# Two attentions interleaved in one stream, with 32-wide PE tiles and side work placed by a list scheduler

## Chip, cores and metric

One core of one Trainium2 chip. The metric is the device time of one execution in microseconds (us), lower is better. Times are medians of the fast runs or of all runs, as stated; a run counts as slow when it is over 1.5% above the fastest of its kernel. On one core there is no second die to compare with.

The engines: PE (TensorE matmul; PEld is its weight load), ACT (ScalarE), DVE (VectorE), POOL (GpSimd), SP (SyncE, here the queue that issues the DMAs). Matmul results land in a memory called PSUM, which both kernels use as eight banks of 512 columns. PV is the product of the exps with V.

## The reference

Two independent blocks on their own inputs, side by side in the output. S = 2048 tokens, D = 1024, 32 heads of 32.

```python
# A: plain multi-head attention, not causal
q, k, v = split_heads(x @ wqkv)
p = softmax(q @ k.T * 32**-0.5)
a = merge(p @ v) @ wo

# B: four segments of 512 tokens; causal attention inside a segment, and a linear memory across segments
phi = lambda t: where(t > 0, t + 1, exp(t))
for s in range(4):
    a_dot = softmax(qs @ ks.T * scale + causal_mask) @ vs
    a_mem = (phi(qs) @ M) / (phi(qs) @ z + 1e-6)
    o_s   = g * a_mem + (1 - g) * a_dot           # g = sigmoid(beta), one per head
    M += phi(ks).T @ vs ;  z += sum(phi(ks))
b = merge(o) @ wo
out = concat([a, b], -1)
```

The exp is the big job: 32 heads x 2048 x 2048 scores in A and 32 x 4 x 512 x 512, half of them masked, in B. On 128 partitions that is 1.05 M columns for A and 0.16 M for B.

## The kernel before

It runs A to its end, then B. A head group is 4 heads (128 rows of K, Q and V). A unit is one key tile of 128 for two heads: two score matmuls over all 128 rows, with K masked so that only one head's 32 rows count, one exp over 1024 columns, two PV matmuls on 64-column tiles. V carries 32 columns of ones beside its 32, so that PV also gives the sum of the softmax.

```python
def mmS(e):                                        # scores of one unit
    for s_, h in enumerate(heads):                 # two heads, two PSUM banks
        e.matmul(K.psS[:, 1024*sbuf + 512*s_ : ... + nq],
                 KTm[:, h, P*t:P*t+P],             # K with the other heads' rows zeroed: 128 rows
                 QT[:, c_q0:c_q0+nq], start=True, stop=not causal)
    if causal: ...                                 # two more matmuls add the mask
...
e.activation(dst, src, ACT.Exp, bias=cb[:, t:t+1], scale=scale)
...
e.matmul(K.psOL[64*s_:64*s_+64, col:col+nq], VE[:, t, h, 0:64], K.PT[:, pb, ...],
         start=first_t, stop=last_t, tile_position=(0, 64*s_))
```

Projections and norms of the next head group are spread over the first two of a group's four query chunks by a fixed share per unit. At the end of a chunk the sums are permuted by matmuls, inverted by one wide reciprocal and multiplied in:

```python
cpl = self.pe_op(... K.perm[:, 2+p, :] ...)        # sort the sums' rows
c2 = self.dve_op(lambda e: e.reciprocal(K.rec[:, 0:nq], K.Lsb[:, 0:nq]), ...)   # 128x512
c3 = self.dve_op(lambda e: e.tensor_tensor(OT_dst, K.Osb[:, 0:nq], K.rec[:, 0:nq], ALU.mult), ...)
```

B's phase starts only after A's last output projection, and loads its input then.

## Time and profile before

| | before |
|---|---|
| time, median of 2 runs | 2339.85 us (2338.29 to 2341.41) |
| PE / DVE / ACT / POOL busy | 74 / 44 / 57 / 0% |
| granted PE clock, mean | 0.884 |
| A's exps, from first to last | about 62 to 1346 us |
| B | about 1420 to 2280 us |

The span in 40 equal slices of 58.5 us (second part of the profile page). Each digit is the busy share of a slice in tenths; PEclk is the granted clock of PE in tenths:

```profile
PE   4888888788788788888878884657657574756659
...
ACT  0678788788788696887899900343342424243330
...
PEclk9999999999999998999999997768677686867779
```

ACT is busy in A (slices 2 to 23) and mostly idle in B. The table of windows (columns: window, its length, busy us and number of instructions of PE, PEld, DVE, ACT and POOL, granted clock, DMA share, GB/s) puts numbers to a pure stretch of A and to B:

```profile
360.00:385.00 25.00, 21.13 (x102) 4.54 (x98) 1.29 (x2) 25.00 (x27) 0.00 (x0) 1.00 0.00 1
1420.00:2280.00 860.00, 530.19 (x3666) 275.43 (x3667) 604.83 (x856) 293.20 (x424) 0.00 (x0) 0.75 0.06 12
```

In A's pure stretch ACT is busy all of its 25 us. In B no engine is: DVE leads with 605 of 860 us, at a PE clock of 0.75.

The timeline of a pure stretch of A (columns: start, us, engine, line of the kernel, operation, output and input, count, then the idle time before it and what ended it):

```profile
298.85 8.19 ACT L533 ACTIVATE PT<-psS,cb_A 128x1024 bf16<-128x1024 f32 x8
...
300.06 0.60 PE L505 MATMUL psS<-QT_A,KTm_A 128*128 128x512 bf16 x2 [0.31 <-ACT PT L533]
...
300.59 0.62 PE L547 MATMUL psOL<-PT,VE_A 128*64 128x512 bf16 x4
...
302.06 0.61 PE L505 MATMUL psS<-QT_A,KTm_A 128*128 128x512 bf16 x2 [0.31 <-ACT PT L533]
```

One period of two units runs from 300.06 to 302.06, so a 1024-column exp costs 1.00 us when they stand back to back. PE needs about 1.7 us of those 2.0. The chain of work that ended last, as shares of the span by engine and by line, for the whole kernel:

```profile
DVE 20%; PE 17%; ACT 6%; issue 3%; SPq 1%; DMA 1%; ACTq 0%; DVEq 0%
PE psX L669 4%; ACT PT L533 4%; DVE rec L619 3%; PE psS L505 3%; DVE drec_B L1022 3%; PE psX L328 3%; PE psOL L547 1%; ACT OLsb L603 1%; PE psS L510 1%; PE psX L608 1%; DVE zp_B L906 1%; DVE KTm_B L858 1%; DVE VE_B L471 1%; DVE VE_B L473 1%; DVE V_B L469 1%
```

The two lines name only half of the span, because the chain has very many short pieces. The head of it is spread over DVE, PE and ACT, and the reciprocals L619 and L1022 of B stand among its largest single lines.

### The profile page before, as it was taken

To read this page: it belongs to the slowest core of one execution; us is meant where nothing else is said; L and a number is where in the kernel's file an instruction comes from. 1 tells how busy PE (TensorE), PEld (TensorE's weight loads), DVE (VectorE), ACT (ScalarE), POOL (GpSimd) and SP (SyncE) were. 2 spreads that over 40 slices of the span, in tenths; PEclk is the share of its full clock that TensorE was granted. 3 is DMA by queue.
4 is the path that set the end of the run, shared out by engine and by line. 5 is a ranking of instruction groups with operands and counts; after the bars stand their busy time and mean duration, and the time that the engine had idled before them with its cause. 6 is when DMAs were issued, how large, how long until landed. Compare 5 with 4: busy or idle time off the path is not lost. (4 is left out here: it accounts for less than half of the span.)

```text
span 2339.9 us, 25486 instructions
## 1 busy us (share of the span) xinstructions
PE 1743.0 (74%) x10128; PEld 663.7 (28%) x10128; DVE 1020.6 (44%) x1373; ACT 1345.2 (57%) x1458; POOL 10.4 (0%) x44
## 2 busy tenths in 40 slices
PE   4888888788788788888878884657657574756659
PEld 2332222222222222322211131433324242332324
DVE  3322312332222314223122142666767676776783
ACT  0678788788788696887899900343342424243330
POOL 1000000000000000000000000000000000000000
PEclk9999999999999998999999997768677686867779
DMA  7000000000000000000000015000000000000002
GB/s 171 14 14 1 1 14 1 1 14 1 1 14 1 1 14 1 1 1 1 1 0 1 1 59 113 14 1 14 14 0 14 0 14 1 14 1 1 1 1 72
DMA packets 95702, 35.20 MB, mean 15 GB/s; under 512 B 85344, under 2 KB 93536, under 8 KB 95584
## 3 DMA queue, kind: packets, MB, share of 16 engines
q1 hardware_dynamic: 95584, 33.57, 6.3%
q8 instruction: 81, 1.33, 0.2%
q14 instruction: 37, 0.30, 0.0%
HBM read 16.78 MB, written 8.39 MB: 11 GB/s over the span
## 5 line engine op out<-in xcount | busy, mean ns | idle before, releaser
L533 ACT ACTIVATE PT<-psS,cb_A 128x1024 bf16<-128x1024 f32 x1024 | 1048.7, 1156 | 230.3 <-PE psS L505 203.9
L505 PE MATMUL psS<-QT_A,KTm_A 128*128 128x512 bf16 x2048 | 598.9, 390 | 114.0 <-ACT PT L533 112.9
L533 ACT ACTIVATE PT<-psS,cb_B 128x1024 bf16<-128x1024 f32 (+3 forms) x256 | 188.2, 789 | 399.6 <-PE psS L510 399.5
L547 PE MATMUL psOL<-PT,VE_A 128*64 128x512 bf16 x2048 | 323.4, 396 | 4.8 <-ACT PT L533 4.8
L505 PEld LDWEIGHTS psS<-QT_A,KTm_A 128*128 128x128 bf16 x2048 | 138.5, 99 | 499.6 <-ACT PT L533 446.1
L634 DVE CAST OLsb<-psOL 128x1024 bf16<-128x1024 f32 x32 | 39.1, 1221 | 440.4 <-PE psOL L547 440.4
L505 PE MATMUL psS<-QT_B,KTm_B 128*128 128x512 bf16 (+3 forms) x512 | 143.4, 378 | 46.8 <-ACT PT L533 46.6
L328 PE MATMUL psX<-xT_B,Wsl 128*128 128x512 bf16 x512 | 130.4, 402 | 45.5 <-DMA Wsl<-in_B_wv_dram 26.8
L328 PE MATMUL psX<-xT_A,Wsl 128*128 128x512 bf16 x512 | 132.0, 386 | 28.2 <-DMA Wsl<-in_A_wqkv_dram 26.3
L547 PEld LDWEIGHTS psOL<-PT,VE_A 128*64 128x64 bf16 x2048 | 73.2, 109 | 227.8 <-issue 218.1
L471 DVE TENSOR_TENSOR VE_A<-psX,fcol_A 128x512 bf16<-128x512 f32 x32 | 22.1, 691 | 244.3 <-PE psX L368 244.3
L650 DVE RECIPROCAL rec<-rec 128x512 f32<-128x512 f32 x32 | 107.0, 3343 | 0.0
L619 DVE RECIPROCAL rec<-rec 128x512 f32<-128x512 f32 x32 | 107.0, 3343 | 0.0
L1016 PE MATMUL psX<-PQ_B,Zb_B 128*128 128x512 bf16 x24 | 12.6, 527 | 96.4 <-DVE Zb_B L1012 96.4
L510 PE MATMUL psS<-maskneg,ident 128*128 128x128 bf16 x512 | 82.9, 256 | 0.0
L1022 DVE RECIPROCAL drec_B<-drec_B 128x512 f32<-128x512 f32 x24 | 80.5, 3353 | 0.8
L328 PEld LDWEIGHTS psX<-xT_B,Wsl 128*128 128x128 bf16 x512 | 47.4, 102 | 117.7 <-issue 40.5
L603 ACT ACTIVATE OLsb<-psOL 128x1024 bf16<-128x1024 f32 x32 | 32.7, 1023 | 77.6 <-PE psOL L547 77.6
L368 PE MATMUL psX<-Wsl,xT_A 128*128 128x128 bf16 x1024 | 76.3, 234 | 0.6 <-DVE rec L642 0.6
L368 PE MATMUL psX<-Wsl,xT_B 128*128 128x128 bf16 x1024 | 72.7, 238 | 5.1 <-DVE drec_B L1019 2.5
L675 DVE CAST outsb<-psX 128x512 bf16<-128x512 f32 x64 | 44.1, 691 | 73.1 <-PE psX L669 64.3
L368 PEld LDWEIGHTS psX<-Wsl,xT_A 128*128 128x128 bf16 x1024 | 64.7, 105 | 29.0 <-issue 18.5
(123 smaller groups left out, 1484.0 us busy)
## 6 DMA issues: line engine op xcount, KB each, us to landing
out_dram<-outsb SPq DMA_DIRECT2D x64, 128.0 KB, 1.7
Wsl<-in_A_wqkv_dram SPq DMA_DIRECT2D x24, 256.0 KB, 4.4
Wo_A<-in_A_wo_dram SPq DMA_DIRECT2D x1, 2048.0 KB, 10.4
Wo_B<-in_B_wo_dram SPq DMA_DIRECT2D x1, 2048.0 KB, 15.3
Wsl<-in_B_wk_dram SPq DMA_DIRECT2D x8, 256.0 KB, 3.3
Wsl<-in_B_wq_dram SPq DMA_DIRECT2D x8, 256.0 KB, 4.1
Wsl<-in_B_wv_dram SPq DMA_DIRECT2D x8, 256.0 KB, 4.5
xT_A<-in_A_x_dram SPq DMA_TRANSPOSE x8, 5.0
```

Source lines behind the costliest of these rows:

```text
L328: ins = e.matmul(K.psX[:, 512 * b:512 * b + ncol], K.Wsl[Wb][:, i, blk, :], xT[:, i, ncol * c4:ncol * c4 + ncol], start=(i == 0), stop=(i ...
L368: ins = e.matmul(K.psX[:, 512 * b + 128 * tt:512 * b + 128 * tt + 128], xT[:, i, P * t:P * t + P], K.Wsl[Wb][:, i, blk, :], start=(i == 0) ...
L505: ins = e.matmul(K.psS[:, 1024 * sbuf + 512 * s_:1024 * sbuf + 512 * s_ + nq], KTm[:, h, P * t:P * t + P], QT[:, c_q0:c_q0 + nq], start=Tr ...
L510: ins = e.matmul(K.psS[:, 1024 * sbuf + 512 * s_:1024 * sbuf + 512 * s_ + P], K.ident[:, :], K.maskneg[:, :], start=False, stop=True)
L533: attE(e.activation(dst, src, ACT.Exp, bias=cb[:, t:t + 1], scale=scale))
L547: ins = e.matmul(K.psOL[64 * s_:64 * s_ + 64, col:col + nq], VE[:, t, h, 0:64], K.PT[:, pb, 512 * s_:512 * s_ + nq], start=first_t, stop=l ...
L603: c1 = self.act_op(lambda e: e.activation(K.OLsb[:, :, 0:nq], K.psOL[:, :].rearrange("p (a n) -> p a n", a=2)[:, :, 0:nq], ACT.Copy), wait ...
L619: c2 = self.dve_op(lambda e: e.reciprocal(K.rec[:, 0:nq], K.Lsb[:, 0:nq]), waits=[(sd, cl)])
L634: c1 = self.dve_op(lambda e: e.tensor_copy(K.OLsb[:, :, 0:nq], K.psOL[:, :].rearrange("p (a n) -> p a n", a=2)[:, :, 0:nq]), waits=waits)
L650: c2 = self.dve_op(lambda e: e.reciprocal(K.rec[:, 0:nq], K.Lsb[:, 0:nq]), waits=[(sd, cl)])
L675: cd = self.dve_op(lambda e, b=b, ob=ob: e.tensor_copy(K.outsb[:, ob, :], K.psX[:, 512 * b:512 * b + 512]), waits=wd)
L1022: cd2 = self.dve_op(lambda e: e.reciprocal(drec[:, 0:L], drec[:, 0:L]), waits=[(sd, cd1)])
```

## The change

The intent is to keep ACT fed from one end to the other: B's units, one after each unit of A, so that B's serial chains run under A's exps; less PE time for scores; exps of up to 1536 columns; and side work placed into the gaps by a list scheduler that plays the program with estimated costs when it is built. The order that it finds is static: every engine then works through its list and waits on semaphores.

The diff replaces nearly the whole file. Its core, shortened and partly put in words, with cuts marked by `...`:

```diff
-for pair in range(2): for t in range(NT): unit(two heads)      # A, then all of B
+for n in range(32):                                              # A and B alternate
+    units.append(("B", n) + ...)
+    units.append(("A", n) + ...)

+SLOTS = [(0, 1, 2), (3, 4)]     # score banks: groups of 3 and of 2
+PROJ = [5]                      # the one side bank
+OB, LB = 6, 7                   # PV output, softmax sums

-ins = e.matmul(psS..., KTm[:, h, ...], QT[...])                  # 128 rows, masked K
+hs = slice(32 * h, 32 * h + 32)
+lhsT = self.KA[b][hs, P*t:P*t+P]; rhs = self.QA[b][hs, ...]      # 32-row tiles, one head each
+ACT: activation(PT[:, s0:s0+n, 0:width], ps[:, banks[0]:banks[0]+n, 0:width], Exp, bias=cb, scale=SCALE)   # n = 2 or 3

-e.matmul(K.psOL[64*s_:64*s_+64, ...], VE[:, t, h, 0:64], ...)    # 64-column tiles, V and ones together
+for ones in (False, True):
+    for h in range(4):                                           # 32-column tiles, four heads
+        e.matmul(ps[32*h:32*h+32, LB if ones else OB, ...], ones32 or V[:, t, hs], PT[...])

-# causal mask by two matmuls; bias of the softmax by matmuls, a diagonal and DVE reductions
+POOL: affine_select(PT...)                                       # causal mask after the exp
+POOL: partition_all_reduce(cbB[:, 1:2], ..., ReduceOp.max)       cost=1.0
+POOL: tensor_scalar(cbB[:, 0:1], cbB[:, 1:2], -SCALE, ...)       cost=0.2
+POOL: tensor_tensor(Mb, Mf, maskbd); tensor_scalar(Zb, maskbd, z)    # state operands of B's memory

-reciprocal of 128x512
+four reciprocals of 128x128, so that other DVE work can come between

+def proj_T(...):
+    bank = yield ("bank",)                 # a free side bank
+    for i0 in range(0, NI, 2):
+        yield ("pe", 0)                    # a gap on PE
+        R.op("PE", two matmuls, ..., cost=0.45)
+    op = R.op("DVE", copy out of the bank, ..., cost=0.66)
+    self.bank_release(bank, op)
+# scheduler: scores first, then PV, then the side task of the best priority
...
```

Loads also change: B's weights are loaded once for each of its 32 units and B's input in four parts.

## The prediction

> **What bounds the kernel now.** It runs two attentions one after the other. In A's pure attention stretches (timeline, 360 to 385 us) ScalarE is saturated: busy 25.00 of 25 us. Its 1024-column exp has a mean of 1156 ns in the groups view, but two start every 2.01 us, so it costs 1.003 us: by that, about 0.83 ns a column plus 0.15 us an instruction (my fit). 1024 of them need 1027 us, and A takes 1285 us (60 to 1345): the loss is PE side work (projections stretch two units to 2.39 us, timeline) and gaps of 3 to 6.5 us at chunk ends and norm chains (waits). Then 56 us of output projection and 26.8 us of waiting for B's loads idle ScalarE. B (1420 to 2280) is bound by serial chains: in the table of windows DVE is busy 72%, ScalarE 36%, PE 64% at a granted clock of 0.75; the chain of waits runs through reciprocals (3.34 us each), the wide reductions and PE.
>
> **What the change does.**
> - B's exps fill under A's. Exp columns stay 1.05 M (A) + 0.16 M (B). With 3+2 banks there are about 26 instructions per A unit and 5 per B unit: ScalarE's floor is 31x0.15 us + 38000 columns x 0.83 ns = 36.2 us per A+B pair, with phi's exp about 37, or 1190 us for 32 pairs.
> - Scores: four masked 128-row matmuls per key tile (0.216 us each) become four 32-row matmuls that should overlap; groups of 2 or 3 cost about 0.25 us. The Trainium skill, TensorE: Matmul & The Clock Gate, Part 3, gives 3.07x for four row tiles of N=512; this trace has no row tiles.
> - PV keeps its PE time, about 0.45 to 0.55 us per key tile: before, four 64-column matmuls take 0.55 us in the timeline (two overlap); now eight of 32 columns, four overlapping.
> - Gone: KTm masks, VE scaling, permutation matmuls, mask matmuls, diagK chain, relu. DVE falls to about 800 us; affine selects move to POOL (0.29 us per 128 columns in the trace).
> - Added: PE mode switches, about 0.1 us each from the trace (four PV matmuls take 0.55, not 0.43), some 60 to 70 a pair; one side bank, held until DVE's 0.69 us copy ends, about 20 uses a pair.
>
> **Sum.** PE per pair: scores 7.6, PV 9.3, side 16 (48 projection matmuls of 0.216, 64 of 0.06, norms, memory, output), switches 7: about 40 us, above ScalarE's 37. PE becomes the bound, ScalarE close behind. Static order and the single bank add some: 43.5, or 1392 us. Start: both inputs' transposes (issue 2.34 us each for A) and the first A preparation through one bank, about 80 us before A's first exp. Tail: last output projections, about 35 us. Total 1510 us.
>
> **Predicted: 1510 us, 1410 to 1620 (8 in 10). Faster by over 2%: 0.97; within 2%: 0.01; slower: 0.02.**
>
> **Right or wrong shows in:** exp instructions about 990, with PE 80% or more busy and clock above 0.93 throughout; ScalarE occupied 75 to 85%; its idle ended mostly by PE scores; DVE 50 to 60%; side matmuls waiting for the DVE copy of the one bank.
>
> **What would make it wrong:** row or column tiles not overlapping (scores then over 1 us per key tile, above 1700 us); switches cheaper than 0.1 us (toward 1400); POOL's partition all-reduce taking many us and holding masks and the bias; a static order that fits the engines badly, so PE waits in order.

## The result and the profile after

| | before | after |
|---|---|---|
| time, median of 2 runs | 2339.85 us | 1697.27 us (1689.94 to 1704.60) |
| ratio of fast runs | | 0.7253, interval 0.7178 to 0.7328 |
| PE / DVE / ACT / POOL busy | 74 / 44 / 57 / 0% | 78 / 47 / 71 / 9% |
| granted PE clock, mean | 0.884 | 0.917 |

A ratio is the mean time of one kernel's fast runs over that of the other's fast runs of the same rounds, so it is not quite the ratio of the medians. The change is a large gain, but the 1697 us lie above the stated range of 1410 to 1620.

The span in 40 slices of 42.6 us:

```profile
PE   0478878887788776898678868788688878788976
...
ACT  0138959995889562997679946599479958498920
...
PEclk9899979997989798889879998899889999898999
```

ACT is now busy throughout, but not evenly: nearly full slices alternate with slices at 4 to 7. The chain, by engine and by line:

```profile
ACT 55%; PE 22%; issue 9%; DVE 8%; SPq 2%; DMA 2%; POOL 1%; another core or an unknown queue 0%; POOLq 0%; ACTq 0%; DVEq 0%
ACT PT L392 54%; PE ps L505 6%; PE ps L710 4%; PE ps L444 4%; PE ps L380 4%; PE ps L522 2%; DVE outsb L717 2%; DVE Ls L464 2%; SPq L306 1%; SPq L293 1%; DMA out_dram<-outsb 1%; DVE KQB L508 1%; DMA beta<-in_B_beta_dram 1%; DVE cbB L610 1%; DVE VA L527 1%
```

The 9% of "issue", about 155 us in which an engine on the chain waited for nothing that the profile shows, was not there to this size before (3%). The table of windows, cut at the first exp of A and at the last exp, divides the time into a start, a middle and a tail:

```profile
0.00:112.80 112.80, 44.76 (x310) 20.59 (x313) 25.16 (x44) 7.47 (x8) 8.25 (x27) 0.94 0.41 91
112.80:1627.00 1514.20, 1228.16 (x11039) 417.55 (x11173) 746.04 (x1120) 1193.49 (x1018) 142.85 (x333) 0.91 0.11 27
1627.00:1703.00 76.00, 49.73 (x206) 18.10 (x210) 23.34 (x33) 0.00 (x0) 0.00 (x0) 0.97 0.12 45
```

| | predicted | measured | difference |
|---|---|---|---|
| start, up to A's first exp | 80 | 112.8 | +33 |
| middle, 32 pairs | 1392 (43.5 each) | 1514.2 (47.3 each) | +122 |
| tail, after the last exp | 35 | 76 | +41 |

The PE pieces of the sum held. In a stretch where the stream flows (timeline of PE alone):

```profile
840.85 0.39 PE L380 MATMUL ps<-QA,KA 32*128 32x512 bf16 x2
841.16 0.40 PE L444 MATMUL ps<-PT,VA 128*32 128x512 bf16 x4
841.39 0.39 PE L444 MATMUL ps<-PT,ones 128*32 128x512 bf16 x4
841.71 0.60 PE L505 MATMUL ps<-xB,WB 128*128 128x512 bf16 x2
842.25 0.39 PE L380 MATMUL ps<-QA,KA 32*128 32x512 bf16 x3
842.57 0.40 PE L444 MATMUL ps<-PT,VA 128*32 128x512 bf16 x4
```

Groups of 2 and 3 scores take 0.31 and 0.32 us, including the change of tile shape (840.85 to 841.16 and 842.25 to 842.57). Four V matmuls take 0.23 us and four of ones 0.32 with the change after them: the four column tiles run side by side. With 31 score groups and about 18.5 key tiles a pair that is 31 x 0.315 + 18.5 x 0.55 = 20 us, where the prediction had 7.6 + 9.3 and most of the 7 for switches, so these pieces were set somewhat too high.

What the prediction did not have is this. One stretch of the timeline of all engines, where B's unit follows A's:

```profile
809.67 0.69 DVE L508 CAST KQB<-ps 128x512 bf16<-128x512 f32 x1 [2.07 <-PE ps L505]
...
810.39 1.06 ACT L631 ACTIVATE E<-KQB 128x1024 bf16<-128x1024 bf16 x1 [12.59 <-DVE KQB L508]
...
813.36 0.38 POOL L613 PARTITION_ALL_REDUCE cbB<-cbB  x1 [6.19 <-issue]
...
814.25 0.55 PE L380 MATMUL ps<-KQB 32*128 32x512 bf16 x5
...
821.04 0.26 POOL L615 TENSOR_SCALAR cbB<-cbB 128x1 f32<-128x1 f32 x1 [7.31 <-issue]
821.39 2.54 ACT L392 ACTIVATE PT<-ps,cbB 128x1024 bf16<-128x1024 f32 x2 [9.95 <-POOL cbB L615]
```

B's K and Q come at 809.67, its scores are issued at 814.25, and the all-reduce is on record for 0.38 us at 813.36. But the next instruction of POOL, a multiply of 128 numbers by a constant, starts at 821.04 after 7.31 us of "issue". It makes the bias of the exp, and the exp starts at 821.39. (The 6.19 us of issue before the all-reduce are the same kind of gap on the way to it, most of it hidden behind work that the all-reduce had to wait for anyway.) ACT had nothing to do from 797.8 to 821.4 but one exp of phi. The list of waits sums this up (columns: engine, what, line, the releaser; total us, times, longest):

```profile
POOL cbB L615 <- issue: 226.0, 32, 8.0
...
ACT PT L392 <- POOL cbB L615: 141.2, 14, 17.6
...
ACT E L631 <- DVE KQB L508: 135.7, 9, 24.3
...
ACT PT L392 <- PE ps L380: 97.0, 67, 39.8
```

POOL loses 7.06 us each of 32 times after the all-reduce (226.0 / 32), and as much after each of A's eight all-reduces (cbA at L566: 56.9 us in 8 places). ACT waits 141 us for the bias. It waits another 136 us, 9 times, where an exp of phi stands in its list ahead of K and Q that are late.

At the start, the timeline shows a chain of small things:

```profile
36.00 2.06 SPq L314 DMA_DIRECT2D beta<-in_B_beta_dram  x4
...
50.86 1.28 ACT L345 ACT_TABLE_LOAD   x1 [50.86 <-DMA beta<-in_B_beta_dram]
...
52.92 0.68 DVE L508 CAST KQB<-ps 128x512 bf16<-128x512 f32 x1
...
53.66 0.61 PE L505 MATMUL ps<-xB,WB 128*128 128x512 bf16 x1 [37.44 <-DVE KQB L508]
```

The four loads of beta, 0.5 KB each, were issued at 36 us, behind all of A's transposes. A step that needs the sigmoid of beta (L346) stands first in DVE's list, so the copy that would free the side bank waited behind it until 52.92, and PE with it. The Trainium skill, TensorE: Matmul & The Clock Gate, section "Architectural detail", says that VectorE's queue is strictly in order; this trace agrees, at a price of 37.44 us of idle PE.

At the tail the timeline shows the output projections of A through the one side bank:

```profile
1692.14 1.90 PE L710 MATMUL ps<-xA,OTA 128*128 128x512 bf16 x8 [0.79 <-DVE outsb L717]
1694.08 0.69 DVE L717 CAST outsb<-ps 128x512 bf16<-128x512 f32 x1 [2.00 <-PE ps L710]
...
1694.82 1.90 PE L710 MATMUL ps<-xA,OTA 128*128 128x512 bf16 x8 [0.79 <-DVE outsb L717]
```

A half projection every 2.68 us, of which PE sits idle 0.79 until DVE's copy has freed the bank. 22 of A's 32 half projections were still to do after the last exp, behind 3 of B's, because their tasks have the lowest priority.

### The profile page after: what moved, and what is told of

The parts are those of the page before. It is cut to its first block, busy times and chain, and to the rows that moved or that the text cites. A ratio compares the mean times of both kernels' runs of the same rounds, so it can differ in the third digit from the quotient of the medians.

```text
span 1702.9 us, 26458 instructions
## 1 busy us (share of the span) xinstructions
PE 1322.7 (78%) x11551; PEld 456.2 (27%) x11696; DVE 794.5 (47%) x1196; ACT 1201.0 (71%) x1026; POOL 151.1 (9%) x360
## 4 chain that ended last, share of the span: by engine, by line
ACT 55%; PE 22%; issue 9%; DVE 8%; SPq 2%; DMA 2%; POOL 1%; another core or an unknown queue 0%; POOLq 0%; ACTq 0%; DVEq 0%
ACT PT L392 54%; PE ps L505 6%; PE ps L710 4%; PE ps L444 4%; PE ps L380 4%; PE ps L522 2%; DVE outsb L717 2%; DVE Ls L464 2%; SPq L306 1%; SPq L293 1%; DMA out_dram<-outsb 1%; DVE KQB L508 1%; DMA beta<-in_B_beta_dram 1%; DVE cbB L610 1%; DVE VA L527 1%
## 5 line engine op out<-in xcount | busy, mean ns | idle before, releaser
L392 ACT ACTIVATE PT<-ps,cbA 128x1024 bf16<-128x1024 f32 (+1 forms) x832 | 1012.4, 1384 | 83.7 <-PE ps L380 83.3
L380 PE MATMUL ps<-QA,KA 32*128 32x512 bf16 x2048 | 337.5, 402 | 81.9 <-ACT PT L392 62.1
L392 ACT ACTIVATE PT<-ps,cbB 128x768 bf16<-128x768 f32 (+3 forms) x160 | 171.5, 1173 | 155.6 <-POOL cbB L615 141.2
L444 PE MATMUL ps<-PT,ones 128*32 128x512 bf16 (+3 forms) x2560 | 250.0, 387 | 0.0
L464 DVE RECIPROCAL Ls<-Ls 128x128 f32<-128x128 f32 x256 | 241.8, 945 | 2.8
L505 PE MATMUL ps<-xB,WB 128*128 128x512 bf16 x469 | 145.2, 427 | 97.8 <-DVE KQB L508 44.8
L444 PE MATMUL ps<-PT,VA 128*32 128x512 bf16 x2048 | 207.9, 396 | 1.4 <-ACT PT L392 0.9
L380 PEld LDWEIGHTS ps<-QA,KA 32*128 32x128 bf16 x2048 | 79.6, 91 | 409.3 <-ACT PT L392 366.8
L505 PE MATMUL ps<-xA,WA 128*128 128x512 bf16 x459 | 134.7, 402 | 17.7 <-issue 7.6
L415 POOL TENSOR_SCALAR_AFFINE_SELECT PT<-PT 128x512 bf16<-128x512 bf16 (+3 forms) x208 | 93.4, 464 | 368.1 <-ACT PT L392 365.6
L380 PE MATMUL ps<-KQB 32*128 32x256 bf16 (+3 forms) x512 | 61.4, 342 | 66.8 <-ACT PT L392 63.6
L657 DVE RECIPROCAL den<-den 128x128 f32<-128x128 f32 x96 | 91.4, 952 | 3.0
```

The costliest lines, as they stand in the source:

```text
L380: ins = e.matmul(o, l, r, start=True, stop=True)
L392: op = R.op("ACT", lambda e: e.activation(self.PT[:, s0:s0 + n, 0:width], self.ps[:, banks[0]:banks[0] + n, 0:width], ACTF.Exp, bias=cb, s ...
L415: mo = R.op("POOL", lambda e, ap=ap, pat=pat: e.affine_select(ap, ap, pattern=pat, compare_op=ALU.is_ge, fill=0.0, base=0, channel_multipl ...
L444: ins = e.matmul(o, l, r, start=(st == 0), stop=stop)
L464: R.op("DVE", lambda e, cs=cs: e.reciprocal(Ls[:, cs], Ls[:, cs]), r=[("Ls", x)], w=[("Ls", x)], cost=0.9)
L505: ins = e.matmul(self.ps[:, bank, :], W[:, i, :], xsl(i), start=(i == 0), stop=(i == NI - 1))
```

## The experiments

Two theories of the middle at first. Theory 1: the all-reduce's hidden latency stands on the critical path. Theory 2: the one side bank is too slow for the side work, B's preparation is late for that reason, and the all-reduce only shows it. They were tested together with the two ends. Fifteen kernels ran, in four calls of 3 or 4, each call on one chip with its own runs of the kernel before; all results were correct.

### The changed kernel again

> The changed kernel itself, as the yardstick of this chip and these rounds. Every theory expects 1690 to 1705 us, a ratio to before of about 0.725, the first exp of attention A near 113 us, the last exp near 1627 us.

Measured: 1698.64, 1699.13 and 1694.59 us, ratio 0.7255 (0.7243 to 0.7267). A fourth run, the profiled one, took 3722.89 us with a recorded clock of 1.000 and PE busy 96%, its matmuls more than twice as long (894 against 402 ns for A's scores). What happened there is not known, and no other run showed it.

### The bias without the all-reduce

```diff
-POOL: partition_all_reduce(cbB[b][:, 1:2], cbB[b][:, 1:2], P, ReduceOp.max)
+POOL: tensor_scalar(cbB[b][:, 1:2], cbB[b][:, 1:2], 0.0, None, ALU.mult)      # and the same for A's two columns
```

> The POOL all-reduce of the softmax bias is replaced by a POOL multiply by zero: same order of every engine, same dependencies, only its hidden 7 us gone (softmax does not change with the bias, so the result stays right). Theory 1, the all-reduce latency sits on the critical path of about every second B unit: the wait of ScalarE for the bias (141 us now) falls under 30 us and the time by 90 to 140 us, to 1560 to 1610. Theory 2, the side work through the one side bank is the limit and the all-reduce only shows where it is behind: ScalarE then waits for PE scores or for K and Q instead, and the time falls by less than 50 us.

Measured: 1595.42 us, ratio 0.6826 (0.6814 to 0.6838): 102 us less than the changed kernel beside it, by the means of the fast runs. The order of every engine is the same, since the scheduler was told the same costs. The issue share of the chain fell from 9 to 1%, and the wait for the bias is gone from the list. The middle, between the same events, from the table of windows:

```profile
106.40:1515.10 1408.70, 1207.94 (x11174) 411.92 (x11173) 745.65 (x1120) 1188.35 (x1018) 138.17 (x333) 0.96 0.12 29
```

The middle is 1408.7 us, 44.0 a pair, close to the predicted 43.5; the tail, 74.6 us, is as it was. The same matmuls also take less PE time, 1208 us and not 1228 (and the trace of the changed kernel lacks 135 of these 11174), at a granted clock of 0.96 and not 0.91. The Trainium skill, TensorE: Matmul & The Clock Gate, Part 1, says that PE falls to half rate after some 3.4 us of idleness. The changed kernel's trace agrees, in the one gap that was looked at: by the table of windows the granted clock is 1.00 from 806 to 811 us, 0.78 in the gap from 814.8 to 820.2, 0.50 from 820.2 to 828 and 0.99 from 828 to 830. In the slow part four PV matmuls start 0.40 us before the next four, against 0.23 us in the flowing stretch above:

```profile
820.16 0.63 PE L505 MATMUL ps<-xB,WB 128*128 128x512 bf16 x1 [5.36 <-DMA xB<-in_B_x_dram]
...
824.47 0.62 PE L444 MATMUL ps<-PT,VB 128*32 128x512 bf16 x4
824.87 0.64 PE L444 MATMUL ps<-PT,ones 128*32 128x512 bf16 x4
```

A DMA of B's input ended this gap, not POOL, so it shows the slow clock and not what brought it. Where PE waited for ACT before the scores (L380), the longest wait fell from 5.7 us to 1.5 without the all-reduce, and the sum from 125.7 to 71.9 us. That fits the higher mean clock, but how much of the gain came by way of the clock was not separated.

So taking the all-reduce away is worth 105 us in the middle and 6 at the start, between two profiled runs that lie 113 us apart; by the medians it is 103 us in all.

### Two side banks in place of one

```diff
-SLOTS = [(0, 1, 2), (3, 4)]
-PROJ = [5]
+SLOTS = [(0, 1), (2, 3)]
+PROJ = [4, 5]
```

> Score banks 2+2 and two side banks in place of 3+2 and one; everything else kept, the scheduler orders anew. Theory 2, the single side bank starves the preparation: B units are prepared in time, the all-reduce is hidden, the tail shrinks, and the time falls by 120 us or more, to under 1580, although ScalarE has about 3 per cent more exp time (37 exps a pair, not 31). Theory 1: the all-reduce still stands before each B unit, and the time falls by less than 60 us.

Measured: 1599.83 and 1620.89 us in the two fast runs (1632.13 and 1632.37 in two that count as slow), ratio 0.6883 (0.6830 to 0.6935), so 87 us less by the means of the fast runs. That is between what the two theories expected. The exps are 38 a pair (1216 in all), one more than the expectation said. ACT's wait for the bias was still 87 us in 12 places, and the issue share of the chain 8%.

### Both ends mended

```diff
 def loads(self):
+    four loads of beta                     # first of all, no longer behind A's transposes
 ...
+if cur >= len(self.units):                 # all scores are out
+    self.proj += the five score banks      # the output projections may use them
```

> Two ends at once, each read by itself in the trace: the four tiny beta loads are issued first, and once the last scores are out the output projections may use the five score banks too. The first exp of attention A should come 15 to 35 us earlier than the 113 us of the changed kernel; from the last exp to the end should take 45 to 60 us and not 76. The middle should keep its pace of about 47 us a pair. Time lower by 35 to 60 us, about 1645.

Measured: 1653.84 us, ratio 0.7061 (0.7030 to 0.7093), 45 us less. A's first exp came at 92.2 us (20.6 earlier), the tail lasted 50.4 us (25.6 less), and the middle kept 46.8 us a pair. The preparation of A's first group, through the one bank, is what is left of the start.

### Ends and bias together

> Both the zeroed bias and the two mended ends. If the three causes are independent, the gains add: 1699 minus 103 minus 45 is about 1550 us (1535 to 1570): first exp of A near 86 us, middle near 44 us a pair, 50 us from the last exp to the end.

Measured: 1557.09 us, ratio 0.6647 (0.6635 to 0.6658). The first exp of A came at 92.9 us, not 86: at the start the two gains overlap, since the first preparation of A now ends the wait. The middle and tail add up as expected.

### Two side banks, with nothing to hide

> Score banks 2+2, two side banks, and the bias zeroed. Theory 1 (two side banks only helped by preparing early enough to hide the all-reduce): with nothing to hide they give nothing, and the extra exps cost 25 us: 1580 us or more. Theory 2 (one side bank starves the preparation by itself): 1550 us or less, middle under 42 us a pair.

Measured: 1499.17 us, ratio 0.6404 (0.6395 to 0.6414): 96 us less than with the zeroed bias alone (which ran on another chip; by the ratios to the kernel before, 0.6826 to 0.6404, it is 6% as well).

```profile
104.10:1447.70 1343.60, 1263.39 (x11090) 413.88 (x11091) 738.76 (x1105) 1221.59 (x1240) 136.00 (x313) 0.96 0.12 29
1447.70:1498.00 50.30, 43.36 (x200) 17.72 (x197) 22.04 (x32) 0.01 (x1) 0.00 (x0) 1.00 0.19 69
```

The middle falls from 44.0 to 42.0 us a pair, the tail from 75 to 50 us, and PE is busy 94% of the middle. Theory 1's expectation, that two side banks only hide the all-reduce, has fallen: the one side bank costs its own 65 us in the middle and 24 in the tail, in spite of 7 more exps a pair (1216 and not 992 in all). Both causes are real. Only the all-reduce was missing from the prediction's middle, though: with one bank and no all-reduce the pace is the predicted one within 0.5 us a pair (how far that is luck is said below).

### The all-reduce twice

```diff
+POOL: partition_all_reduce(cbB..., max)    # once more
 POOL: partition_all_reduce(cbB..., max)
```

> The all-reduce of each B unit done twice in a row (idempotent, the result stays right), same order. If its latency is on the path, some 7.5 us more for at least the 14 units that waited and at most all 32: 105 to 240 us more than the changed kernel, so 1800 to 1940. If it is hidden or refilled by other waits, less than 50 us more.

Measured: 1707.11 us, ratio 0.7297 (0.7264 to 0.7329): 9 us more than the changed kernel by medians, hardly clear of the noise (the intervals touch), where 105 to 240 were expected. Theory 1 as it was put has fallen. The timeline of POOL tells why:

```profile
857.71 0.38 POOL L613 PARTITION_ALL_REDUCE cbB<-cbB  x1 [32.11 <-DVE cbB L610]
858.19 0.35 POOL L615 PARTITION_ALL_REDUCE cbB<-cbB  x1
866.15 0.26 POOL L617 TENSOR_SCALAR cbB<-cbB 128x1 f32<-128x1 f32 x1 [7.61 <-issue]
```

The second reduce follows the first by 0.48 us, and the 7.61 us of issue stand after both, once. So it is not the reduce that is slow. The list of instructions by source line has, for the multiply behind the reduce, the following (columns: line, queue or engine, operation, count: shortest, median and longest ns; first and last start in us), for the changed kernel:

```profile
L615 POOLq MODIFY_POOL_CONFIG  x64: 82/83/83, 60.1 to 1546.2; - x64
L615 POOL TENSOR_SCALAR cbB<-cbB x32: 260/260/646, 67.3 to 1553.0; 128x1 f32<-128x1 f32 x32
```

POOL's sequencer changes its configuration 64 times at this line, the first at 60.1 us, 0.4 us after the first all-reduce began; the multiply then starts at 67.3. The Trainium skill, GPSIMD Engine Reference, section 2.1, says that the first call of a freshly loaded routine pays a load of about 6 us with no instruction visible for it. This trace agrees in size: where the change before B's all-reduce was not hidden, POOL idled about 6.2 us (25.0 us in 4 places), and the multiply after the all-reduce pays 7.06 us on average for the way back. Theory R, then: it is the change back that costs 7 us, whichever POOL instruction comes next. The last part of it did not hold, as the final experiment shows.

### The scheduler told the true cost

```diff
-partition_all_reduce(...), cost=1.0
+partition_all_reduce(...), cost=8.0
```

> Same work; the scheduler is told 8 us for the all-reduce in place of 1. If the loss was a wrong order that a right number mends, half of the 103 us comes back: 1650 us or less. If the order has nothing to put there, because K and Q themselves come late through the one side bank, the time stays within 30 us of 1699.

Measured: 1655.92 us, ratio 0.7074 (0.7053 to 0.7094): 43 us less, somewhat under half of the 103 us that bias_zero gained. A wrong number in the schedule is a part of the loss, but with one side bank the scheduler has not enough to put in the gap: ACT still waits 129 us for the bias, in 14 places.

### The multiply moved to VectorE

```diff
-POOL: tensor_scalar(cbB[:, 0:1], cbB[:, 1:2], -SCALE, None, ALU.mult)
+DVE:  tensor_scalar(cbB[:, 0:1], cbB[:, 1:2], -SCALE, None, ALU.mult)     # for A, add and multiply in one
```

> The all-reduce stays on POOL; only the tiny multiply after it (for A, the add and multiply) moves to VectorE. Theory R, the 7 us are POOL's change of configuration after the all-reduce (doubling the reduce cost 8 us in all, so the reduce itself is cheap): the bias comes early, ScalarE's wait for it falls from 141 us to under 40, and the time falls to 1600 to 1660; part may be given back where B's causal masks, still on POOL, wait for the change back. Theory N, the result of the all-reduce itself lands 7 us late: no change, 1690 or more.

Measured: 1704.22 us, ratio 0.7273 (0.7247 to 0.7298): no gain at all, though theory R's mechanism is there. The waits:

```profile
POOL Mb L641 <- issue: 121.2, 17, 7.9
...
DVE den L649 <- PE ps L647: 85.0, 23, 10.7
...
DVE cbB L613 <- POOL cbB L611: 42.4, 32, 6.9
```

VectorE gets the maximum 1.3 us after it is ready to (42.4 us in 32 places), so the result of the all-reduce is not late, and ACT's wait for POOL is gone. But now B's state operand, the next thing in POOL's list, waits 121.2 us in 17 places; the matmul that needs it stands in PE's list and holds the one side bank, and VectorE waits 85.0 us for its result, which was 23.4 us in the changed kernel. ACT's wait for PE's scores rose from 97.0 to 226.0 us. The issue share of the chain is still 7%. The gain was given back at the next POOL instruction of this kind.

### Three combinations

A floor with the zeroed bias, two side banks and both ends:

> Zeroed bias, banks 2+2 with two side banks, and both ends mended: a floor for what the order of this program can reach. 1499 minus about 20 at the start and 5 to 10 at the end: 1465 to 1485 us, with the middle at 42 us a pair.

Measured: 1464.31 and 1476.29 us in the fast runs, 1488.07 and 1488.85 in two that count as slow; ratio 0.6281 (0.6250 to 0.6311).

A real bias made by PE and VectorE instead of POOL:

```diff
-POOL: partition_all_reduce(max); tensor_scalar(-SCALE)
+PE:   matmul(ps[:, bank, 0:1], ones[128x128], mxB[:, 0:1])        # sum of the 128 maxima, an upper bound
+DVE:  tensor_scalar(cbB[:, 0:1], ps[:, bank, 0:1], -SCALE / 16)
```

> A version meant to be kept: as the one before, but with a real bias, made by a PE matmul of ones that sums the per-partition maxima (an upper bound of the maximum; the softmax does not change). 5 to 20 us above the zeroed one: 1475 to 1500, faster than both kernels.

Measured: 1482.23, 1518.35, 1522.47 and 1548.50 us, at granted clocks of 0.968, 0.937, 0.934 and 0.908. Only one counts as fast, so there is no interval.

The multiply on VectorE with two side banks:

> The other way to keep a real bias: POOL's all-reduce with the scaling on VectorE, banks 2+2, both ends mended. Under theory R 1480 to 1530, the masks waiting for POOL at times; under theory N over 1560.

Measured: 1625.53 us, ratio 0.6949 (0.6904 to 0.6994). It fell short of theory R's 1480 to 1530 for the same reason as before: the state operand waits 120.9 us in 17 places for POOL, and PE's list waits behind it.

### Only the masks left behind the all-reduce

```diff
-POOL: tensor_tensor(Mb, Mf, maskbd); tensor_scalar(Zb, maskbd, z)
+DVE:  tensor_tensor(Mb, Mf, maskbd); tensor_scalar(Zb, maskbd, z)         # on top of scale_on_dve
```

> As scale_on_dve, and the two small state operands (the masked M and z of attention B) are made on VectorE too, so that after the all-reduce only B's causal masks are left on POOL. Theory R (7 us of configuration change hit whichever POOL instruction comes next): in scale_on_dve they hit the state operands, which waited 121 us in 17 places and held PE's matmul and the one side bank; now they hit only the masks, and most of the 100 us appears: 1590 to 1640 us, and issue time on the chain falls from 7 per cent to under 4. If the time stays above 1680, the loss is not this wait.

Measured: 1620.93 us, ratio 0.6918 (0.6904 to 0.6932), 83 us less than the version that moved only the multiply (on another chip; the ratios to the kernel before are compared). The issue share of the chain is 1%. VectorE's wait at L649 is down to 20.8 us. The middle takes 44.8 us a pair. The all-reduce is still there 40 times, so it is not what cost the time. But the masks do not pay in place of the multiply, as theory R and the expectation had it. The trace of this run, by source line and in POOL's timeline:

```profile
L611 POOLq MODIFY_POOL_CONFIG  x2: 11/11/11, 12.2 to 12.2; - x2
...
1470.81 0.35 POOL L611 PARTITION_ALL_REDUCE cbB<-cbB  x1 [0.63 <-DVE cbB L608]
1471.04 1.92 POOL L415 TENSOR_SCALAR_AFFINE_SELECT PT<-PT 128x384 bf16<-128x384 bf16 x3
```

A mask (an affine select) follows the all-reduce here with no gap. POOL's configuration changes at the first all-reduce and at no later one, where the changed kernel has 160 such records at its all-reduces and at the instructions behind them. After the setup, POOL's long gaps of issue (over 3 us) stand in all runs either before an all-reduce (5.7 to 6.9 us) or before a TENSOR_SCALAR or TENSOR_TENSOR that follows an all-reduce or a mask (6.6 to 8.0 us), and none stands before a mask. So this version did not hide the change: it left on POOL only instructions that need none between them, and the change is gone.

> The same with banks 2+2 and both ends mended. Theory R: within 30 us of the version with the PE sum, 1480 to 1530; otherwise near 1620, as scale_dve_2_2_start_tail.

Measured: 1480.70 us, four runs from 1479.29 to 1484.45, ratio 0.6330 (0.6320 to 0.6339). This version keeps the exact bias and beats both kernels: 37% less than before, 13% less than the change. Its middle:

```profile
400.00:1400.00 1000.00, 929.72 (x8313) 313.36 (x8410) 615.70 (x970) 909.42 (x926) 84.08 (x173) 0.98 0.13 31
```

PE is busy 930 of 1000 us and ACT 909, at a clock of 0.98. PE and ACT now bound it together, much as the prediction had said of the change (PE the bound, ACT close behind), though the chain of this run goes 73% through ACT and 18% through PE.

> The version with the PE sum, word for word, on another chip: its four runs lay at 1482 to 1548 with granted clocks of 0.968 down to 0.908. If the spread goes with the chip, it is narrower or elsewhere here; if it belongs to the kernel, the runs again spread over some 50 us and the time falls with the clock. 1475 to 1550.

Measured: one fast run of 1480.89 us and five from 1507.46 to 1529.17, at clocks from 0.973 to 0.931, on another chip. The spread is there on both chips, so it is not one chip's. In the profiled run ACT waits for PE scores 158.5 us in 109 places, against 115.1 in 63 in the version just before; why this order makes the clock and the time vary so was not found.

## Why the prediction was wrong, and where it was right

Right, by the trace: exps run 992 times (832 and 160; about 990 predicted). The 32-row and 32-column tiles overlap, and scores, PV and switches take 20 us a pair. ACT is busy 37.1 us a pair in the middle of bias_zero (about 37). DVE falls to 794 us (about 800). B's chains run under A's exps; the one reciprocal among the largest lines of the chain, L464, is down to 2%. Side matmuls wait for DVE's copy of the one bank. With one bank and without POOL's change of configuration the pace is 44.0 us a pair with the bias zeroed and 44.8 with the real one (43.5). That this is so close is partly luck: in bias_zero PE is busy 37.7 us a pair and not 40, and the waiting makes up 6.3 and not 3.5.

Wrong, the step: "Static order and the single bank add some: 43.5, or 1392 us." This term left out POOL. "POOL's partition all-reduce taking many us and holding masks and the bias" stood only among the things that would make the prediction wrong, with no number in the sum. The runs show 105 us for it in the middle and 6 at the start (bias_zero against after). The mechanism is more precise than the words: the reduce itself takes under 0.5 us, and what costs is the change of POOL's configuration after it, 7 us before the next TENSOR_SCALAR or TENSOR_TENSOR on POOL (double_reduce, scale_on_dve). With masks alone behind the all-reduce there is no change and most of the loss is gone (reduce_masks_pool). Part of it is that the scheduler had been told 1 us (true_cost, 43 us). The one side bank, which makes K and Q late, is a part too, but not the whole: with two banks ACT still waited 87 us for the bias and not 141 (banks_2_2).

Two more terms were mis-sized. Start: 80 predicted, 112.8 measured. Loading beta first gives 20.6 us of it back, the all-reduce is 6.4, and the two overlap. Tail: 35 predicted, 76 measured. The prediction let only the last chunk's projection stand after the last exp; in fact 22 of A's 32 half projections and 3 of B's stood there, one every 2.68 us through the one bank. Five more banks took 25.6 us off.

The three together: 33 + 122 + 41 = 196 us, which is the difference between the terms 80 + 1392 + 35 and the profiled run.

Of what the prediction named to look for, four failed: PE was busy 78% (in a trace that lacks 145 of 11696 matmuls) and not 80 or more, at a clock of 0.917 and not above 0.93; ACT was occupied 71%, not 75 to 85; DVE 47%, not 50 to 60; and ACT's idle time was ended by POOL (141 us) and by late K and Q (136 us) more than by PE's scores (97 us). In bias_zero, with the change of configuration gone, all four hold, three of them narrowly: PE 82% at a clock of 0.959, ACT 75%, DVE 50%, and PE's scores end the most of ACT's idle time (139 us, late K and Q 129).

## What to carry to other kernels

When a change brings an instruction of a kind that the old trace does not have, put a number for it into the sum, not only among the risks, and ask what stands behind it on the same engine: here the instruction took 0.4 us and its neighbour paid 7, and what helped was to leave no neighbour of that kind on the engine. A static order built from estimated costs is as good as its worst estimate on the critical path, so compare its costs with the first trace, line by line. A move that frees one wait must be followed to the next instruction in the same list: the gain was given back there until that one moved too.

## What the Trainium skill lacked or had wrong

- GPSIMD Engine Reference, section 2.1: it has the load on the first call of a freshly loaded routine, about 6 us. It does not say that a TENSOR_SCALAR or TENSOR_TENSOR after a partition all-reduce pays such a change as well, every time: 7.06 us on average, 32 times (226.0 us), with two all-reduces in a row paying it once. Nor does it say that an affine select after an all-reduce pays none: one started within 0.23 us of the start of an all-reduce (reduce_masks_pool). Before the all-reduce the change is usually hidden, since it is issued ahead of the wait (at 5.1 us for the first reduce at 59.7); where it was not, it cost about 6.2 us (25.0 us in 4 places).
- TensorE: Matmul & The Clock Gate, Part 3: it gives 3.07 times for four row tiles and 2.38 for three column tiles, and no figure for four column tiles. In a flowing stream four 32-column tiles of N=512 took 0.23 us, and one matmul in a stream takes 0.216 (a group of 8 in the output projections of before every 1.73 us), so 4 x 0.216 / 0.23 is 3.8 times. This is a rate in a stream, and no run here has three column tiles to compare.
- TensorEngine Tiling (Array Packing), Key Properties: it says that a change of tiling mode drains the engine, but gives no cost. Here a score group of two took 0.31 us with the change, 0.09 above the 0.216 of one matmul; by that difference the change costs about 0.09 us (an estimate).
